# Folding the tokens a second time ahead of the channel DFT in an attention and Fourier-mix kernel

## Chip, cores and metric

The kernel runs on one core of a Trainium2 chip. The metric is the time of one execution on the device, in microseconds (us). The kernel before took 1283.77 us, the median of three runs (1283.46 to 1284.94).

## What is computed

Two blocks follow one another: attention with a hash mask, then a Fourier mix (FNet) with a small MLP. Cut to what matters:

```python
# attention, B, H, S, D = 4, 8, 768, 64; 6 hash bits
mask = q_bucket[..., :, None] == k_bucket[..., None, :]      # same hash bucket only
attn = softmax(where(mask, q @ k.T * scale, -1e9)) @ v

# bridge: (B, H, S, D) -> x of (B, S, 512)
X = fft(fft(x, axis=1), axis=2)                               # over tokens, then channels
u = x + real(X)
un = (u - mean(u)) / sqrt(var(u) + 1e-6)                      # over the 512 channels
out = u + maximum(un @ w_ch1, 0) @ w_ch2                      # 512 -> 2048 -> 512
```

The real part of the double transform needs sums with cosines and sums with sines only. Both are symmetric, so rows and columns can be added or subtracted in pairs ("folded") before a matmul, which makes the matmul smaller.

## The kernel before

The mix of batch b runs beside the attention of batch b + 1. Both are written as generators. An attention step (24 in a batch, 6 key blocks for each of 4 pairs of heads) is followed by three pieces of the mix. Batch 0's attention is emitted in a fixed order; later batches are ordered by a scheduler at compile time, which prefers what comes earlier in the program and fills an engine's gaps with later work. So the order of emission is a priority, and within one engine the final order is fixed at compile time. The mix of batch 3 has nothing beside it.

```python
def attention(b):
    ...
    for t in range(NPAIR):                       # 4 pairs of heads
        ...
        accs = [wt([P, 2, HALF], F32, "t3", f"acc{n}_{g}", 3) for g in range(2)]
        for c in range(NT):                      # 6 blocks of 128 keys
            new = [weigh(n, g, c) for g in range(2)]    # sc matmul, exp (ScalarE), mask (VectorE): pk
            if c == 0:
                first = new
            else:
                for g in range(2):               # the row sums: acc = pk + pk, acc + pk
                    nc.vector.tensor_tensor(accs[g], first[g][...] if c == 1 else accs[g], new[g][...], op=ALU.add)
            while pending:
                finish()                         # oo matmuls of the step before; after c = 5 the scaling of x
            ...
            yield

def mix(b):
    x = xs[b]
    z = wt([P, 2, 2, 2, HALF], F32, "z", f"z{b}", 1)
    for cp in range(2):                          # four pieces of fold
        for pc in range(2):
            e = wt([P, S], F32, "t3", f"e{b}_{cp}_{pc}", 3)
            nc.vector.tensor_tensor(e, x[:, cp], x[:, cp + 2], op=ALU.subtract if pc else ALU.add)
            for par in range(2):                 # s with s + 384: even and odd frequencies
                nc.vector.tensor_tensor(z[:, cp, pc, par], e[:, 0:HALF], e[:, HALF:S],
                                        op=ALU.subtract if par else ALU.add)
            yield
    hd = DM // 2
    F = wt([P, 2, NT // 2, 4 * hd], F32, "F", f"F{b}", 1)
    for par in range(2):
        for t in range(NT // 2):                 # channel DFT, 3 row blocks
            ps = pt([P, DM], f"cs{b}_{par}_{t}")
            for pc in range(2):
                for cp in range(2):
                    nc.tensor.matmul(ps[:, pc:DM:2], z[:, cp, pc, par, t * P : (t + 1) * P],
                                     ch[:, cp, pc, :], start=(cp == 0), stop=(cp == 1))   # 256 columns
            nc.scalar.copy(f[:, 0:DM], ps)
            nc.vector.tensor_copy(...)           # the mirrored half, read backwards
            yield
    ...
    for j in range(NDC):                         # sequence DFT
        pa, pb = (pt([P, HALF + 1], f"{nm}{b}_{j}") for nm in "AB")
        for par in range(2):
            for k, ps in enumerate((pa, pb)):
                for t in range(NT // 2):         # 3 row blocks
                    nc.tensor.matmul(ps[:, cols], f, sq[:, t, k, cols],
                                     start=(t == 0), stop=(t == NT // 2 - 1))
        ...                                      # x += A, x += or -= B
        yield
    ...                                          # h = relu(x @ w1), un (transposes), o = h @ w2

for b in range(B):
    if b > 0:
        for _ in attention(b):
            for _ in range(per_step):            # 3
                next(other, None)
    ...
    for _ in other:
        pass
    other, per_step = mix(b), 3
```

In what follows a piece is what runs from one `yield` of the mix to the next.

## Time and profile before

| | before |
|---|---|
| median of three runs | 1283.77 us |
| span of the profiled run | 1283.1 us |
| mean granted TensorE clock | 0.987 |
| idle time of TensorE (span less busy) | 61.5 us |

The page has a line with the granted clock in 40 slices of 32 us, in tenths of full speed (9 is 90% or more). This is the line of before:

```profile
PEclk9988999999999999999999999999999998999999
```

Every stretch of the clock in this trace is at 0.5 or 1.0, so an 8 is a slice with a few us at half clock. There are two in the first 130 us and one near 1080 us, after the last attention, and none beside the attention of batches 1 to 3. (A 9 can still hide a short stretch: the trace has half clock from 225.8 to 229.3.)

### The profile page before, as it was taken

The page shows a single profiled execution, that of the slowest core. Times are in us where ns is not written, and L with a number is a line of the kernel's source. Part 1 is how long each engine was busy: PE and PEld are TensorE (multiplying, and loading weights), DVE is VectorE, ACT ScalarE, POOL GpSimd, SP SyncE. Part 2 cuts the span into 40 slices and gives each one's busy share as a digit, 9 for nine tenths or more (in the row PEclk, how much of TensorE's full clock was granted, in tenths as well). Part 3 has the DMA queues.
Part 4 walks back from the last instruction along what each step waited for, and adds up shares of the span by engine and source line. Part 5 has one row for each costly group of instructions (what it writes and reads, how often), then busy time and mean ns, then how long its engine had stood idle before and what let it go on. Part 6 is the DMA issues. An engine that isn't in the chain of part 4 may idle for free.

```text
span 1283.1 us, 12028 instructions
## 1 busy us (share of the span) xinstructions
PE 1221.6 (95%) x4675; PEld 615.9 (48%) x4675; DVE 646.0 (50%) x1114; ACT 369.5 (29%) x631; POOL 129.8 (10%) x184
## 2 busy tenths in 40 slices
PE   6878898999999999999999999999999998999997
PEld 3333365444454446554455445744445444854553
DVE  3988888734446366443454448554434635311110
ACT  6875558521222132221222214122111211000000
POOL 2543015201001000000000100000000010001000
PEclk9988999999999999999999999999999998999999
DMA  9421225201101110010100101010000000000000
GB/s 291 115 63 38 50 78 168 61 6 29 33 1 25 29 33 14 13 25 9 33 21 13 33 9 46 1 25 13 21 17 1 1 17 9 1 1 17 9 8 19
DMA packets 82881, 44.65 MB, mean 35 GB/s; under 512 B 76800, under 2 KB 76928, under 8 KB 82688
## 3 DMA queue, kind: packets, MB, share of 16 engines
q1 hardware_dynamic: 74032, 23.61, 7.5%
q0 software_dynamic: 5648, 19.40, 4.7%
q10 hardware_dynamic: 3136, 0.79, 0.3%
q8 instruction: 39, 0.64, 0.2%
q14 instruction: 26, 0.21, 0.1%
HBM read 37.50 MB, written 6.29 MB: 34 GB/s over the span
## 4 chain that ended last, share of the span: by engine, by line
PE 78%; DVE 12%; DMA 3%; ACT 3%; issue 3%; POOL 0%; SPq 0%; ACTq 0%; POOLq 0%; DVEq 0%
PE h L974 25%; PE o L1002 25%; PE sc L789 9%; PE oo L809 7%; DVE pk L798 3%; PE cs L923 3%; DVE acc L868 3%; PE B L949 2%; PE A L949 2%; DMA zraw<-in_moe_w_ch_dram 2%; ACT pk L795 1%; PE sum L826 1%; DVE w L595 1%; PE un L990 1%; PE trk L701 1%
## 5 line engine op out<-in xcount | busy, mean ns | idle before, releaser
L974 PE MATMUL h<-x,w 128*128 128x384 f32 x1024 | 343.2, 492 | 9.2 <-DVE rt L832 3.9
L1002 PE MATMUL o<-w,h 128*128 128x512 f32 x768 | 342.1, 597 | 0.4 <-DVE h L981 0.4
L798 DVE SCALAR_TENSOR_TENSOR pk<-qb,kb,pk 128x384 f32<-128x384 bf16 x288 | 169.3, 626 | 194.1 <-ACT pk L795 194.1
L974 PEld LDWEIGHTS h<-x,w 128*128 128x128 f32 x1024 | 191.9, 191 | 156.4 <-issue 12.0
L795 ACT ACTIVATE pk<-sc 128x768 f32<-128x768 f32 x192 | 147.7, 808 | 310.3 <-PE sc L789 223.0
L1002 PEld LDWEIGHTS o<-w,h 128*128 128x128 f32 x768 | 141.5, 190 | 174.2 <-issue 167.7
L789 PE MATMUL sc<-qt,kt 64*128 64x384 f32 x768 | 187.5, 518 | 4.4 <-ACT pk L795 4.4
L809 PE MATMUL oo<-pk,vn 128*64 128x384 f32 (+1 forms) x768 | 157.5, 501 | 0.8 <-DVE pk L798 0.8
L868 DVE TENSOR_TENSOR acc<-acc,pk 128x768 f32<-128x768 f32 x128 | 133.3, 1052 | 10.1 <-ACT pk L795 8.3
L981 DVE TENSOR_SCALAR h<-h 128x384 f32<-128x384 f32 x64 | 35.6, 557 | 176.2 <-PE h L974 175.9
L789 PEld LDWEIGHTS sc<-qt,kt 64*128 64x128 f32 x768 | 76.7, 190 | 80.6 <-issue 50.2
L983 ACT ACTIVATE h<-h 128x384 f32<-128x384 f32 x64 | 31.3, 489 | 285.5 <-PE h L974 285.5
L809 PEld LDWEIGHTS oo<-pk,vn 128*64 128x64 f32 x768 | 48.9, 136 | 95.4 <-issue 79.2
L1008 DVE SCALAR_TENSOR_TENSOR u<-o,rs,u 128x512 f32<-128x512 f32 x24 | 18.0, 751 | 150.8 <-PE o L1002 122.5
L998 POOL TENSOR_SCALAR rs<-mv 128x1 f32<-128x1 f32 x24 | 6.5, 271 | 547.0 <-DVE mv L996 546.6
L893 POOL DMA_DIRECT2D out_dram<-u x32 | 19.6, 614 | 355.2 <-DVE u L1008 301.6
L923 PE MATMUL cs<-ch,z 128*128 128x256 f32 x192 | 47.7, 402 | 5.3 <-DVE z L910 3.7
L992 ACT COPY u<-un 128x512 f32<-128x512 f32 x24 | 14.1, 587 | 114.7 <-PE un L990 114.7
L923 PEld LDWEIGHTS cs<-ch,z 128*128 128x128 f32 x192 | 36.9, 199 | 17.9 <-DVE z L910 4.1
L949 PE MATMUL B<-sq,F 128*128 128x193 f32 (+1 forms) x192 | 37.0, 329 | 1.0 <-DVE F L930 0.6
L949 PE MATMUL A<-sq,F 128*128 128x193 f32 (+1 forms) x192 | 37.5, 330 | 0.0
L868 DVE TENSOR_TENSOR acc<-pk,pk 128x768 f32<-128x768 f32 x32 | 32.0, 1020 | 5.3 <-ACT pk L795 5.0
(109 smaller groups left out, 856.1 us busy)
## 6 DMA issues: line engine op xcount, KB each, us to landing
zraw<-in_moe_w_ch_dram POOLq DMA_DIRECT2D x21, 512.0 KB, 4.3
qn<-in_q_dram SPq DMA_DIRECT2D x32, 192.0 KB, 3.2
vn<-in_v_dram SPq DMA_DIRECT2D x30, 192.0 KB, 3.2
kn<-in_k_dram SPq DMA_DIRECT2D x30, 192.0 KB, 3.2
out_dram<-u POOLq DMA_DIRECT2D x16, 256.0 KB, 2.5
fraw<-in_moe_w_ch_dram SPq DMA_DIRECT2D x4, 512.0 KB, 7.2
fraw<-in_moe_w_ch_dram POOLq DMA_DIRECT2D x4, 512.0 KB, 4.2
out_dram<-u POOLq DMA_DIRECT2D x16, 128.0 KB, 2.4
```

What stands on the lines that cost most here:

```text
L789: nc.tensor.matmul(ps[:, h, 0:HALF], kt[rows, ks], qt[rows, qs], start=kb is not None, stop=True,)
L795: nc.scalar.activation(pk[:, :, 0:HALF], ps[:, :, 0:HALF], AF.Exp, scale=SCALE)
L798: nc.vector.scalar_tensor_tensor(pk[:, h, 0:HALF], qb[:, h, qs], kb[:, h, c : c + 1], pk[:, h, 0:HALF], op0=ALU.is_equal, op1=ALU.mult,)
L809: nc.tensor.matmul(oos[g][h * D : (h + 1) * D, 0:w], nat["v", n][:, c, h, :], pk[g][:, h, 0:w], start=(c == 0), stop=(c == NT - 1),)
L868: nc.vector.tensor_tensor(accs[g], first[g][:, :, 0:HALF] if c == 1 else accs[g], new[g][:, :, 0:HALF], op=ALU.add,)
L893: nc.gpsimd.dma_start(out[b, s0 : s0 + 2 * w - 1 : 2, :], src[at : at + w])
L923: nc.tensor.matmul(ps[:, pc:DM:2], z[:, cp, pc, par, t * P : (t + 1) * P], ch[:, cp, pc, :], start=(cp == 0), stop=(cp == 1),)
L949: nc.tensor.matmul(ps[:, cols], f, sq[:, t, k, cols], start=(t == 0), stop=(t == NT // 2 - 1),)
L974: nc.tensor.matmul(ps, w1[:, c, fc * P : (fc + 1) * P], x[:, c, g * HALF : (g + 1) * HALF], start=(c == 0), stop=(c == NDC - 1),)
L981: nc.vector.tensor_scalar(hr, ps, 0.0, None, op0=ALU.max)
L983: nc.scalar.activation(hr, ps, AF.Relu)
L1002: nc.tensor.matmul(ps, hs[fc][:, j * P : (j + 1) * P], w2[:, fc, :], start=(fc == 0), stop=(fc == NFC - 1),)
```

## The change

The intent is less TensorE work. After the fold of s with s + 384, the tokens are folded once more, s with 384 - s. A sum of cosines over both needs only f(s) + f(384 - s), one of sines only f(s) - f(384 - s). So the cosine rows and the sine rows become separate blocks: the sequence DFT contracts over two row blocks rather than three, and the channel DFT of a block that holds one kind computes 127 to 129 columns, not 256. The price is four small VectorE operations for each of the four fold pieces, with one operand read backwards, and a GpSimd copy of the rows that are their own partners (2 x 2 elements). Half of the fold (cp = 0: pairs 0 and 2) is called at a fixed place in the attention of pair 3; the mix keeps the other half, two pieces.

```diff
 (attention)
+            half = fold(b, 0) if t == NPAIR - 1 else iter(())
-            accs = [wt([P, 2, HALF], F32, "t3", f"acc{n}_{g}", 3) for g in range(2)]
+            accs = [wt([P, 2, HALF], F32, "t3", f"acc{n}_{g}", 4) for g in range(2)]
 ...
                 pending.append((n, c, new, oos, accs))
+                if c > 1:
+                    next(half, None)
 ...
+    def fold(b, cp):
+        x = xs[b]
+        if cp == 0:
+            zs[b] = wt([P, 2, 2, 2, HALF], F32, "z", f"z{b}", 1)
+        for pc in range(2):
+            e = wt([P, S], F32, "t3", f"e{b}_{cp}_{pc}", 4)
+            nc.vector.tensor_tensor(
+                e, x[:, cp], x[:, cp + 2], op=ALU.subtract if pc else ALU.add
+            )
+            f = wt([P, 2, HALF], F32, "t3", f"f{b}_{cp}_{pc}", 4)
+            for par in range(2):
+                nc.vector.tensor_tensor(
+                    f[:, par], e[:, 0:HALF], e[:, HALF:S],
+                    op=ALU.subtract if par else ALU.add,
+                )
+            z = zs[b][:, cp, pc]
+            n = HALF // 4 - 1
+            for at, op in ((0, ALU.add), (2 * n + 3, ALU.subtract)):
+                for i, first, last in ((0, 1, n), (n, 2 * n + 2, n + 1)):
+                    nc.vector.tensor_tensor(
+                        z[:, :, at + i : at + i + last], f[:, :, first : first + last],
+                        turned(f, 2 * n + 1 if i == 0 else HALF - 1, last), op=op,
+                    )
+            nc.gpsimd.tensor_copy(
+                z[:, :, 2 * n + 1 : 2 * n + 3], f[:, :, 0 : n + 2 : n + 1]
+            )
+            yield
 ...
     def mix(b):
         x = xs[b]
-        z = ...                                  # (the fold loop of before)
+        yield from fold(b, 1)
+        z = zs[b]
 ...
+                kinds = (0, 1) if t == 1 else (par ^ (t // 2),)
                 for pc in range(2):
+                    lo = 0 if 0 in kinds else hd // 2 + 1 - pc
+                    hi = hd if 1 in kinds else hd // 2 + 1 - pc
                     for cp in range(2):
                         nc.tensor.matmul(
-                            ps[:, pc:DM:2], z[:, cp, pc, par, t * P : (t + 1) * P],
-                            ch[:, cp, pc, :], start=(cp == 0), stop=(cp == 1),
+                            ps[:, pc + 2 * lo : pc + 2 * hi - 1 : 2],
+                            z[:, cp, pc, par, t * P : (t + 1) * P],
+                            ch[:, cp, pc, lo:hi], start=(cp == 0), stop=(cp == 1),
                         )
 ...
-                    for t in range(NT // 2):
+                    for t in range(2):
                         nc.tensor.matmul(
-                            ps[:, cols], f, sq[:, t, k, cols],
-                            start=(t == 0), stop=(t == NT // 2 - 1),
+                            ps[:, cols], F[:, par, k, t, j * P : (j + 1) * P],
+                            sq[:, t, k, cols], start=(t == 0), stop=(t == 1),
                         )
 ...
-            other = after(NPAIR + NT, other, weights(w2, moe_w_ch2))
+            other = after(2 + NT, other, weights(w2, moe_w_ch2))
```

The tables of constants, the copies into F and the zeroing of F's unused columns are adapted to the new blocks; they are cut here.

## The prediction

> **What bounds the kernel now.** I read, in order: busy times and slices, the groups by line and shape, the matmul timeline of the two stages that the change touches, busy times in short windows around the batch boundaries, and the timeline after the last attention.

> Engine shares, a line of the slices, and the two groups that the change shrinks (A has a twin, B):

> ```profile
> PE 1221.6 (95%) x4675; PEld 615.9 (48%) x4675; DVE 646.0 (50%) x1114; ACT 369.5 (29%) x631; POOL 129.8 (10%) x184
> ...
> DVE  3988888734446366443454448554434635311110
> ...
> L923 PE MATMUL cs<-ch,z 128*128 128x256 f32 x192 | 47.7, 402 | 5.3 <-DVE z L910 3.7
> ...
> L949 PE MATMUL A<-sq,F 128*128 128x193 f32 (+1 forms) x192 | 37.5, 330 | 0.0
> ```

> TensorE is busy 95% of the span, so work taken from it pays wherever nothing else holds that stage. VectorE's 50% is an average: 80 to 90% in the first 220 us, about 10% at the end. Each f32 matmul of the program is two records: the sequence stage issues 4 x 2 x 2 x 3 = 48 matmuls a batch, 192 in four, and A and B have 384 records. Below, "record" means such a half.

> A record's mean duration overlaps its neighbour's, so I take pitches from runs in the timeline:

> ```profile
> 478.26 3.72 PE L923 MATMUL cs<-ch,z 128*128 128x256 f32 x16 [0.21 <-ACT qt L517]
> ...
> 1093.74 1.14 PE L949 MATMUL A<-sq,F 128*128 128x192 f32 x6
> ...
> 1107.59 41.28 PE h L974 x128
> ```

> A record lasts 325 ns, six take 1.14 us, so the pitch is (1.14 - 0.325) / 5 = 0.163 us. The last line, from the chain, gives 41.28 / 128 = 0.3225 us for 384 columns. Both fit columns / 1.2 + 2.5 ns. For 256 columns that makes 216 ns; the trace has (3.72 - 0.38) / 15 = 223.

> Busy times in 5 us windows at the boundary of batches 1 and 2 (columns: TensorE, weight loads, VectorE, ScalarE, GpSimd, clock, DMA):

> ```profile
> 465.00:470.00 5.00, 4.67 (x23) 1.86 (x22) 4.76 (x14) 3.03 (x4) 0.00 (x0) 1.00 0.52 124
> 470.00:475.00 5.00, 5.00 (x24) 1.99 (x22) 5.00 (x10) 0.00 (x0) 0.00 (x0) 1.00 0.27 61
> 475.00:480.00 5.00, 3.59 (x15) 2.04 (x15) 5.00 (x10) 3.54 (x7) 0.00 (x0) 1.00 0.08 17
> 480.00:485.00 5.00, 5.00 (x26) 2.79 (x24) 5.00 (x9) 2.46 (x4) 0.00 (x0) 1.00 0.01 3
> 485.00:490.00 5.00, 5.00 (x21) 3.44 (x20) 4.66 (x8) 2.00 (x4) 0.29 (x2) 1.00 0.35 79
> 490.00:495.00 5.00, 5.00 (x27) 2.81 (x26) 1.63 (x4) 1.40 (x2) 0.00 (x0) 1.00 0.00 0
> ```

> From 465 to 490 VectorE is full: the scaling of pair 3, the fold, the first masks and sums of the next batch. TensorE still has work and loses only some 1.9 us. So the change takes TensorE work, and adds VectorE work, at the one place of a batch where both are near their limit.

> After the last attention nothing runs beside the mix (first TensorE, then VectorE, timeline):

> ```profile
> 1076.66 0.67 PE L923 MATMUL cs<-ch,z 128*128 128x256 f32 x2 [0.95 <-DVE mt L1060]
> 1078.69 1.83 DVE L906 TENSOR_TENSOR e<-x 128x768 f32<-128x768 f32 x2
> 1080.43 1.96 DVE L910 TENSOR_TENSOR z<-e 128x384 f32<-128x384 f32 x4
> 1081.04 10.90 PE L923 MATMUL cs<-ch,z 128*128 128x256 f32 x38 [3.71 <-DVE z L910]
> ```

> Only two e operations stand there, not four. The other two, on pairs 0 and 2, ran during pair 3's attention already (in batch 1 at 401.7 and 407.6, by the operations of tile e): the scheduler had filled VectorE gaps with them. So the "half beside pair 3" moves little; it mostly fixes the place.

> [...] after the 3.71 us wait above, the granted clock was 0.50 from 1081 to 1085. [...]

> **The change, part by part.**

> *Sequence DFT.* Three row blocks become two: 128 of 384 records go, 128 x 0.163 = **20.9 us of TensorE, 5.2 a batch**.

> *Channel DFT.* The pure blocks (two of three) need cosine or sine columns only: 128 of 192 records go from 256 to 127 to 129 columns. By the fit, 216 becomes 109 ns, 128 x 0.107 = **13.7 us, 3.4 a batch**. If weight loads at 190 ns set the pitch, it is only 128 x 0.026 = 3.3 us in all. I believe some 120 ns: 12.3 us, 3.1 a batch.

> *Second fold.* Per (cp, pc): before, e 0.95 and two z of 0.55, 2.05 us. After, e and two f the same, plus four operations on 2 x 95 or 2 x 96 elements, [...] ([...] two measured points give 0.353). Reversed reading seems free: the reversed 510-element F copy takes 687 ns[...]. So 3.47 us, +1.42; with four a batch +5.7, **+22.8 us of VectorE in all**. Half of it lies in pair 3, where VectorE has slack in batches 1 to 3; half at the boundary, +2.8.

> *Evictions.* 16 reversed F copies shrink from 510 to 255 elements, 0.687 to 0.42: -4.3 us VectorE, -1.1 a batch. [...] GpSimd's small copies and memsets stay near 0.2 us each.

> *Buffers and loads.* The table is a third smaller, 1155 to 770 KB, loaded while DMA is saturated: at about 400 GB/s 1 us of DMA, perhaps 0.5 us of time. The third work tile's space becomes a fourth buffer for f.

> TensorE loses 33 to 35 us, 2.6%; if all paid, 1250. By stage I expect less:
> - Batches 1 and 2: VectorE is full for 25 us, and after the change needs 2.8 - 1.1 = 1.7 more there, while the channel DFT waits for a fold that ends later. So the 3.1 us pay 0 to 2, the 5.2 pay. Together 5.5 each, **11**.
> - Batch 0: from 125 to 245 us VectorE, ScalarE and the second weight matrix's load and conversion bind (TensorE idles some 14 us), and part of the second fold delays pair 3 in a fixed order. I give **3** of 8.3.
> - Batch 3: before, last scaled x to first h is 1107.4 - 1078.7 = 28.7 us. After: fold 2 x 3.47 = 6.9, about 4.5 of channel DFT after it, partly at half clock, 64 x 0.163 = 10.4, some 1 of eviction: 22.8. **6**.
> - The mix now has 68 pieces, not 70, for 24 steps at three each, so the last attention step has none: **-1.5** over three batches. Start: **+0.5**.

> Sum 11 + 3 + 6 - 1.5 + 0.5 = 19: 1283.8 - 19 = **1265**.

> **Rivals.** (a) *All of it pays*: 1250. For it: TensorE is 95% busy, and the scheduler can pull later matmuls into gaps. Against it: 25 us of full VectorE, and the matmuls behind it need the whole channel result. (b) *VectorE becomes the bound at the boundaries*: the longer fold delays the channel DFT by all its 2.8 us in four batches and TensorE goes cold; gain 8 to 10, about 1275. For it: full windows and the halved clock after 1081; against: after 490 VectorE drops to a third, so delay is caught up. (c) *The halved channel matmuls are bound by weight loads*: 9 us less TensorE gain, some 3 us less time, 1268. (d) *The fixed fold in pair 3 stalls attention*: [...] the fold blocks it for 3.5 us, twice; four pk buffers hold two steps. In batches 1 to 3 the step has 11 us of other matmuls beside it; in batch 0 it has not, and 2 to 3 us could be lost.

> **Range and chances.** Between (a) and (b), with my sum in the middle: 1254 to 1275. Faster by over 2% means below 1258.1: it needs 26 us, three quarters of all TensorE savings. I give 0.24 to that, 0.75 to within 2%, 0.01 to slower.

> **What would show it.** Sequence matmuls 256 records at pitch 0.163; 128 channel records at 0.11 to 0.13 (0.16 to 0.19 under rival c); small fold operations at 0.35 us; VectorE total some 18 us up, TensorE some 30 down, and TensorE idle up by 10 or more, at the boundaries; the last x to first h at about 23 us. Wrong would be: idle not growing (rival a), or waits of the channel matmuls for z longer than 4 us at each boundary (rival b).

No term of the sum is among them: it came to 11 + 3 + 6 - 1.5 + 0.5 = 19 us, thus 1265. To support its terms, these numbers of before's trace:

- VectorE operations on f32 took 552 ns for 384 elements (z) and 948 for 768 (e). A straight line through both gives 353 ns for the 190 to 192 elements of a small operation, the estimate that still stands; four make 1.41 us, so that +1.42 and 3.47 stay within 0.01, and +22.8 within 0.2. For 255 elements it gives 0.42 us, and for 510 elements 682 ns, beside the 687 of the reversed copy. That reversed reading is free was an estimate at that time.
- The weight loads of A and B last 189 ns each, with the matmuls 163 ns apart, so the two overlap. The "some 120 ns" for a halved channel record is the estimate, between 109 by the fit and 190 by the loads.
- The half clock that goes with the wait of 3.71 us lasts from 1079.2 to 1086.0.
- From 20 to 30 us the DMA moves 410 GB/s at a share of 1.02. The 0.5 us at the start is an estimate, as are the 4.5 us for the channel DFT in batch 3.

## More of the kernel before

The boundary of batches 1 and 2 is where the change acts. VectorE's timeline of before (start, duration, engine, line, operation, tiles, count):

```profile
473.73 1.02 DVE L910 TENSOR_TENSOR z<-e 128x384 f32<-128x384 f32 x2
...
475.20 1.82 DVE L868 TENSOR_TENSOR acc<-pk,pk 128x768 f32<-128x768 f32 x2
...
477.50 0.94 DVE L906 TENSOR_TENSOR e<-x 128x768 f32<-128x768 f32 x1
```

The two parts of the fold that remain at the boundary are split: the first ends with z at 474.7, then come the sums (acc) of the next attention step, and only then the second part.

Last, one 10 us window of batch 0's end in before (columns: TensorE, weight loads, VectorE, ScalarE, GpSimd, clock, DMA share, GB/s):

```profile
140.00:150.00 10.00, 8.24 (x56) 3.51 (x54) 6.08 (x13) 5.14 (x9) 0.00 (x0) 1.00 0.18 40
```

## The result

| | before | after |
|---|---|---|
| median, four runs each | 1283.62 us (1283.19 to 1284.94) | 1280.62 us (1276.26 to 1280.88) |
| ratio | | 0.9967 (95%: 0.9944 to 0.9989) |
| span of the profiled run | 1283.1 us | 1279.0 us |
| mean granted TensorE clock | 0.987 | 0.969 |
| TensorE idle | 61.5 us | 67.9 us |

A ratio is the mean time of one kernel's fast runs over the mean of the other's of the same rounds, so it is not quite the ratio of the medians quoted beside it. The change stayed within 2%, the likeliest of the three outcomes predicted, but its time is 15.6 us above the 1265 predicted and 5.6 us above the top of the range.

The page of after, busy shares, the slices of VectorE and of the clock, and the channel group:

```profile
PE 1211.1 (95%) x4547; PEld 600.3 (47%) x4547; DVE 659.7 (52%) x1178; ACT 368.4 (29%) x639; POOL 145.2 (11%) x188
...
DVE  3988778833536457444444728654344646311110
...
PEclk9988889899999998999999998999999999999999
...
L970 PE MATMUL cs<-ch,z 128*128 128x128 f32 (+3 forms) x192 | 42.8, 381 | 10.6 <-DVE z L944 9.5
```

TensorE has 128 records fewer, as planned, yet its busy time fell only 10.5 us and not the 30 or more expected. The clock line tells why: beside slices 2 and 3 (counted from 0), which before has too, slices 4, 5, 7, 15 and 24 now show an 8. (The half clock after the last attention is still there, now spread over two slices.) A record at half clock takes twice as long and counts as busy all the while: in after the median pitch of 256-column records is 427 ns at 0.5 and 216 at 1.0, that of 384-column records (h) 640 and 323. The channel matmuls' waits for z have grown from 3.7 to 9.5 us.

The stage after the last attention went as foreseen (TensorE's timeline of after):

```profile
1084.90 8.14 PE L970 MATMUL cs<-ch,z 128*128 128x129 f32 x38 [5.11 <-DVE z L944]
...
1094.19 0.81 PE L999 MATMUL A<-sq,F 128*128 128x192 f32 x4
```

The sequence pitch is (0.81 - 0.325) / 3 = 0.162 us. The last scaled x to the first h took 28.7 us before and takes 21.9 us now (1081.4 to 1103.3).

To see where the rest went, I took the ends of the sum matmuls of each batch's pair 3 as marks, and the stretches between them. b0 is batch 0's mark.

| us | start to b0 | b0 to b1 | b1 to b2 | b2 to b3 | b3 to last o |
|---|---|---|---|---|---|
| before | 148.2 | 317.1 | 306.1 | 302.2 | 201.6 |
| after | 153.9 | 318.2 | 304.7 | 300.1 | 194.2 |
| gain | -5.7 | -1.1 | 1.4 | 2.1 | 7.4 |

So the last stage gains 7.4 us, the batch boundaries with attention beside them almost nothing, and batch 0 loses 6.8. The boundary of batches 1 and 2 in after, in 5 us windows with the columns as before:

```profile
475.00:480.00 5.00, 5.00 (x27) 1.93 (x24) 5.00 (x12) 1.46 (x2) 0.00 (x0) 1.00 0.00 2
480.00:485.00 5.00, 2.25 (x10) 0.86 (x8) 5.00 (x14) 0.00 (x0) 4.11 (x2) 1.00 0.00 0
485.00:490.00 5.00, 4.08 (x12) 2.01 (x11) 4.97 (x11) 3.30 (x6) 1.21 (x1) 0.52 0.20 45
490.00:495.00 5.00, 5.00 (x15) 3.93 (x14) 2.02 (x4) 0.90 (x4) 0.00 (x0) 0.50 0.15 34
```

From 480 to 485 TensorE is busy 2.25 of 5 us and ScalarE not at all, with VectorE full. Then the clock falls to 0.50 for ten us (485.2 to 495.5). VectorE's timeline in that window:

```profile
480.74 0.95 DVE L930 TENSOR_TENSOR e<-x 128x768 f32<-128x768 f32 x1
481.60 1.15 DVE L944 TENSOR_TENSOR z<-f 128x190 f32<-128x190 f32 x4
482.68 1.02 DVE L935 TENSOR_TENSOR f<-e 128x384 f32<-128x384 f32 x2
483.61 0.61 DVE L811 SCALAR_TENSOR_TENSOR pk<-qb,kb,pk 128x384 f32<-128x384 bf16 x1
484.14 1.15 DVE L944 TENSOR_TENSOR z<-f 128x190 f32<-128x190 f32 x4
485.21 0.95 DVE L882 TENSOR_TENSOR acc<-pk,pk 128x768 f32<-128x768 f32 x1
```

Here both remaining fold parts stand in a row, and acc comes after both. TensorE meanwhile (the wait before a group and who ended it stand in brackets):

```profile
482.27 0.71 PE L970 MATMUL cs<-ch,z 128*128 128x129 f32 x4 [1.46 <-DVE z L944]
484.28 0.86 PE L822 MATMUL oo<-pk,vn 128*64 128x384 f32 x2 [1.29 <-DVE pk L811]
...
486.67 0.90 PE L714 MATMUL trq<-ident,qn 128*128 128x128 f32 x3 [0.92 <-DVE F L983]
...
490.36 5.37 PE L970 MATMUL cs<-ch,z 128*128 128x256 f32 x16
```

Three waits of 1.46, 1.29 and 0.92 us, all ended by VectorE; the clock falls before the third. The 16 channel records after them take 5.37 us. The emission explains the order. With two fold pieces in place of four, and three pieces per attention step, both fold pieces and the first channel piece fall into the first step of the next batch, ahead of that batch's first acc (step c = 1). In before the last piece of fold fell into the second step, behind that acc.

Adding up the time at half clock, twice (1 - mean clock) times the span, gives 33 us before and 80 us after. The 47 more are worth up to 23 us, half of their length, if TensorE bounds them throughout; 2.7 of the 47 lie after the last work, so up to 22 are left. TensorE's work fell by 128 x 0.163 = 20.9 us and by 128 x some 0.104 = 13.3 us (223 ns before, about 119 now, measured below), in all 34. 34 less up to 22 for the clock and 6.4 for idle time leaves about 6; the span shows 4.1.

Around the end of batch 0's attention (153.9), whose order is fixed, 10 us windows of after:

```profile
140.00:150.00 10.00, 6.50 (x34) 2.64 (x36) 6.53 (x13) 4.08 (x7) 0.38 (x1) 0.69 0.01 3
...
170.00:180.00 10.00, 10.00 (x28) 6.25 (x28) 6.57 (x13) 4.84 (x10) 0.00 (x0) 0.60 0.18 41
```

In the first, TensorE is busy 1.7 us less than before in the same window and the clock halves at 143.9 for 6.8 us; at 167.8 it halves again, for 10.2 us. Before has neither. The second stretch is past b0, at the boundary of batches 0 and 1, and has the same waits for z and pk just before it, of 1.46 and 1.29 us.

### The profile page after: what moved, and what is told of

Its sections match the earlier page's. It is cut to its first block, busy times and chain, and to the rows that moved or that the text cites. A ratio compares the mean times of both kernels' runs of the same rounds, so it can differ in the third digit from the quotient of the medians.

```text
span 1279.0 us, 11866 instructions
## 1 busy us (share of the span) xinstructions
PE 1211.1 (95%) x4547; PEld 600.3 (47%) x4547; DVE 659.7 (52%) x1178; ACT 368.4 (29%) x639; POOL 145.2 (11%) x188
## 4 chain that ended last, share of the span: by engine, by line
PE 80%; DVE 12%; ACT 3%; issue 3%; DMA 1%; POOL 0%; SPq 0%; POOLq 0%; ACTq 0%; DVEq 0%
PE h L1024 25%; PE o L1052 25%; PE sc L802 10%; PE oo L822 8%; PE cs L970 3%; DVE acc L882 3%; DVE pk L811 2%; PE A L999 2%; PE B L999 1%; PE sum L839 1%; ACT pk L808 1%; DVE w L608 1%; PE un L1040 1%; PE trk L714 1%; DMA qn<-in_q_dram 1%
## 5 line engine op out<-in xcount | busy, mean ns | idle before, releaser
L802 PE MATMUL sc<-qt,kt 64*128 64x384 f32 x768 | 196.5, 532 | 0.0
L882 DVE TENSOR_TENSOR acc<-acc,pk 128x768 f32<-128x768 f32 x128 | 132.8, 1052 | 12.3 <-ACT pk L808 10.4
L802 PEld LDWEIGHTS sc<-qt,kt 64*128 64x128 f32 x768 | 79.3, 195 | 77.6 <-issue 51.9
L970 PE MATMUL cs<-ch,z 128*128 128x128 f32 (+3 forms) x192 | 42.8, 381 | 10.6 <-DVE z L944 9.5
L948 POOL COPY z<-f 128x4 f32<-128x4 f32 x16 | 19.9, 1245 | 120.2 <-DVE f L935 120.1
L613 POOL TENSOR_TENSOR w<-w,fraw 128x512 int32<-128x512 int32 x16 | 26.3, 1642 | 63.9 <-DVE w L608 25.8
```

The source lines that it names most:

```text
L613: nc.gpsimd.tensor_tensor(di, di, low, op=ALU.add)
L802: nc.tensor.matmul(ps[:, h, 0:HALF], kt[rows, ks], qt[rows, qs], start=kb is not None, stop=True,)
L882: nc.vector.tensor_tensor(accs[g], first[g][:, :, 0:HALF] if c == 1 else accs[g], new[g][:, :, 0:HALF], op=ALU.add,)
L970: nc.tensor.matmul(ps[:, pc + 2 * lo : pc + 2 * hi - 1 : 2], z[:, cp, pc, par, t * P : (t + 1) * P], ch[:, cp, pc, lo:hi], start=(cp == 0) ...
```

## The experiments

My theory after the two traces: the place of the fold in VectorE's order, fixed by where it is emitted, makes TensorE wait in short bunches; the bunches halve its clock; both together eat the gain. Rivals: the slow GpSimd copy holds z back; the added VectorE time itself does it wherever it stands; the halved channel matmuls gain less than their columns. Twelve kernels were run. All gave correct results. The ratios are against the kernel before, run on the same chip in the same rounds.

| label | what | median us | ratio (95%) | clock |
|---|---|---|---|---|
| (the change) | | 1280.62 | 0.9967 (0.9944 to 0.9989) | 0.969 |
| e1_act_copy | self-paired rows copied by ScalarE | 1279.16 | 0.9961 (0.9945 to 0.9978) | 0.974 |
| e2_no_early_half | both halves of the fold in the mix | 1263.72 | 0.9845 (0.9828 to 0.9863) | 0.983 |
| e3_full_channel | all 256 channel columns | 1287.06 | 1.0018 (1.0001 to 1.0035) | 0.977 |
| e4_hold_four | four pieces held back to the fold | 1248.78 | 0.9723 (0.9707 to 0.9739) | 0.984 |
| e5_pad | two empty pieces ahead of the fold | 1267.05 | 0.9864 (0.9848 to 0.9881) | 0.980 |
| e6_warm | filler matmuls beside the fold | 1271.74 | 0.9902 (0.9886 to 0.9919) | 0.985 |
| e7_noearly_hold4 | e2 and e4 together | 1251.37 | 0.9716 (0.9668 to 0.9764) | 0.981 |
| e8_before_hold4 | before, four pieces held back | 1268.53 | 0.9887 (0.9870 to 0.9903) | 0.989 |
| e9_noearly_hold4_warm0 | e7, fillers in batch 0 | 1248.12 | 0.9717 (0.9701 to 0.9734) | 0.986 |
| e10_noearly_hold8 | e2, eight pieces held back | 1239.81 | 0.9649 (0.9633 to 0.9665) | 0.980 |
| e11_double_small_folds | small fold operations issued twice | 1287.58 | 1.0028 (1.0011 to 1.0044) | 0.975 |
| e12_hold8_warm0_3 | e10, few fillers in batch 0 | 1241.24 | 0.9657 (0.9639 to 0.9675) | 0.986 |

The clock is that of the profiled run. The spans of the profiled runs between the marks (to about 0.1 us, one execution each), which the readings below use:

| us | start to b0 | b0 to b1 | b1 to b2 | b2 to b3 | b3 to last o |
|---|---|---|---|---|---|
| after | 153.9 | 318.2 | 304.7 | 300.1 | 194.2 |
| e1 | 152.0 | 317.9 | 304.7 | 300.1 | 194.2 |
| e2 | 149.2 | 312.7 | 300.5 | 296.5 | 194.5 |
| e3 | 154.2 | 318.2 | 304.3 | 303.5 | 197.1 |
| e5 | 150.9 | 314.6 | 300.4 | 296.5 | 194.5 |
| e6 | 153.2 | 313.0 | 302.7 | 298.2 | 195.1 |
| e11 | 155.5 | 318.9 | 306.4 | 302.2 | 194.4 |

### e1: is it the GpSimd copy?

```diff
-            nc.gpsimd.tensor_copy(
+            nc.scalar.copy(
                 z[:, :, 2 * n + 1 : 2 * n + 3], f[:, :, 0 : n + 2 : n + 1]
```

> Only edit: the copy of the two self-paired rows of z goes from GpSimd to ScalarE. In the changed kernel two such copies took 5.33 us together while VectorE was full. Rival 'GpSimd copy holds the mixed block': the channel matmuls start 2 to 3 us earlier at each of three boundaries, and with them the halved clock is shorter; total 1270 to 1274 us. My theory (VectorE's queue at the boundary and the halved clock after TensorE's idle gap): the channel matmuls wait for the z operations of VectorE, not for the copy, so 1279 to 1282 us, unchanged within 2 us.

Measured: 1279.16 us, 0.9961 beside the change's 0.9967. In after the copy of 128 x 4 elements took up to 2.86 us on GpSimd at the boundaries, and 0.30 to 0.38 in nine of its 16 cases, with VectorE busy beside both; on ScalarE it took 0.20 us at most. Still the stretches from b0 on moved by 0.3 us at most, so at the boundaries the copy is slow but not on the path, and this rival is out there. The stretch before b0 was 1.9 us shorter; whether by the copy or by the clock, which halved at other places, is open.

### e2: is it the place of the fold?

```diff
-            half = fold(b, 0) if t == NPAIR - 1 else iter(())
+            half = iter(())
 ...
+        yield from fold(b, 0)
         yield from fold(b, 1)
 ...
-            other = after(2 + NT, other, weights(w2, moe_w_ch2))
+            other = after(4 + NT, other, weights(w2, moe_w_ch2))
```

> Only edit: both halves of the fold stand in the mix again, none at a fixed place in pair 3. My theory: in batch 0 the fixed order delayed the end of pair 3 by 5.7 us (sum matmuls end at 153.9 instead of 148.2 us) and halved the clock for 6.8 us at 144; without it the end is back at 148 to 149 us. In the later batches the scheduler fills VectorE gaps with the first half as it did before the change, so little moves. Total 1272 to 1278. Rival (the early half helps, VectorE is the bound at the boundary and now gets 7 us more there): 1285 to 1300, with longer waits of the channel matmuls for z.

Measured: 1263.72 us, better than the theory's range. The same arithmetic with the four fold pieces in the mix gains 1.55% on before instead of 0.33%; the early half, with the two pieces fewer in the mix that go with it, costs 1.2%, some 16 us. VectorE's order at the boundary is that of before again:

```profile
472.85 1.81 DVE L882 TENSOR_TENSOR acc<-pk,pk 128x768 f32<-128x768 f32 x2
...
475.14 0.93 DVE L930 TENSOR_TENSOR e<-x 128x768 f32<-128x768 f32 x1
```

TensorE has one longer wait there and no cold stretch after it (timeline; then the window around the wait):

```profile
474.78 0.91 PE L802 MATMUL sc<-qt,kt 64*128 64x384 f32 x2 [2.00 <-ACT pk L808]
...
484.89 2.05 PE L971 MATMUL cs<-ch,z 128*128 128x127 f32 x16
```

```profile
470.00:475.00 5.00, 2.74 (x11) 0.89 (x10) 5.00 (x12) 1.75 (x3) 3.32 (x1) 1.00 0.35 79
```

The clock is 1.00 in this window, and the next three are full, also at 1.00. The run of 16 records also measures the halved channel matmul: (2.05 - 0.27) / 15 = 0.119 us each, with 0.27 for the last one. That is near the predicted 0.12, so the rival that weight loads hold them at 0.16 to 0.19 is out. And the fixed place was not needed for overlap: in e2 the scheduler itself ran the e operations of pairs 0 and 2 at 398.3 and 406.1, in pair 3's gaps.

Against before, e2's stretches gain -1.0, 4.4, 5.6, 5.7 and 7.1 us.

### e5: is it the bunching alone?

e2 moves both halves. Here the early half stays, and only the second half is moved back by two empty pieces:

```diff
+        yield
+        yield
         yield from fold(b, 1)
 ...
-            other = after(2 + NT, other, weights(w2, moe_w_ch2))
+            other = after(4 + NT, other, weights(w2, moe_w_ch2))
```

> Changed kernel with the early half kept in pair 3, and two empty pieces put ahead of the second half in each mix, so that the second half's two parts stand one attention step apart, as in the run without the early half (which gave 1263.7). Theory 'bunching': what cost the later batches was that the mix had two pieces fewer ahead of the second half, so that both its parts fell into the first attention step and delayed the masks and sums of the next; padding heals it: boundaries of batches 1 and 2 without half clock, total 1267 to 1272 (batch 0's delay of pair 3 stays). Rival 'the fixed place in pair 3 itself costs in every batch': total stays at 1277 to 1281.

Measured: 1267.05 us, ratio 0.9864. That is 1.03% of the 1.22% that e2 gains over the change. Two statements without any work take back some 13 of 16 us. VectorE's order at the boundary of batches 1 and 2:

```profile
475.36 1.15 DVE L944 TENSOR_TENSOR z<-f 128x190 f32<-128x190 f32 x4
476.43 1.82 DVE L882 TENSOR_TENSOR acc<-pk,pk 128x768 f32<-128x768 f32 x2
...
478.73 0.93 DVE L930 TENSOR_TENSOR e<-x 128x768 f32<-128x768 f32 x1
```

The sums stand between the two parts again, and neither boundary has half clock. Between b1 and b3 the stretches are those of e2 to 0.1 us; what is left lies in the first two stretches, thus in batch 0, where the early half stands in a fixed order. The empty pieces also move all later pieces of the mix back by two; e5 doesn't part this from the bunch.

### e6: how much of it is the clock?

TensorE is given work that computes nothing of use, 7 matmuls of 384 columns for each batch just ahead of the second half of the fold:

```diff
+        dummy = pt([P, HALF], f"dummy{b}")
+        for _ in range(7):
+            nc.tensor.matmul(dummy, ident, x[:, NPAIR - 1, HALF:S], start=True, stop=True)
         yield from fold(b, 1)
```

> Changed kernel with seven matmuls that compute nothing of use (identity times the scaled half of pair 3, 0.65 us each, 4.5 us of TensorE a batch) ahead of the second half of the fold, where TensorE idles. Theory 'half of the loss is the halved clock': the gap is filled, the clock stays at 1.0 from 485 to 495 us and from 789 to 799, which saves 5 us each, minus 1 to 2 us that the fillers delay others: total 1270 to 1275 though the kernel does more work. Rival (VectorE's queue alone is the cost, the clock only follows): 1280 to 1285.

TensorE's timeline and one window of e6:

```profile
472.26 4.78 PE L957 MATMUL dummy<-x,ident 128*128 128x384 f32 x14
```

```profile
475.00:480.00 5.00, 4.99 (x24) 2.89 (x22) 5.00 (x13) 0.38 (x1) 4.99 (x2) 1.00 0.00 0
```

The fillers add 4 x 14 x 0.3225 = 18 us of TensorE work, and the kernel is some 8 us faster (1271.74 us; 0.9902 against 0.9967). VectorE is as full as in after, the fold parts still stand together, but TensorE has no gaps and keeps its clock. Time at half clock, by the mean clock, falls from 80 to 38 us. No account of the waits alone makes added work pay, so a good part of the loss is the clock. The fillers also shift what stands beside the fold, so the split into waits and clock is not exact.

### e3: what are the halved channel matmuls worth?

```diff
-                    lo = 0 if 0 in kinds else hd // 2 + 1 - pc
-                    hi = hd if 1 in kinds else hd // 2 + 1 - pc
+                    lo = 0
+                    hi = hd
```

> Only edit: the channel matmuls stream all 256 columns again in every block (the sequence stage keeps its two blocks). That gives TensorE 128 records x 0.1 us = 13 us more work. If TensorE were the bound in that stage the total would rise by 10 to 13 us to 1290 to 1294. My theory says that TensorE idles or runs at half clock there, so that this work is nearly free in the three boundaries beside attention and costs about 3 us in the last batch: 1281 to 1286.

Measured: 1287.06 us, 0.5% above the change, thus 6.5 us for 13 us of TensorE work, slightly beyond my range. Two stretches, b0 to b1 and b1 to b2, did not grow at all, but in each of them e3 lacks a stretch of half clock, of 10.2 us, that after has. The window that goes with the cold one of after:

```profile
480.00:485.00 5.00, 2.67 (x12) 1.08 (x8) 5.00 (x14) 0.00 (x0) 3.84 (x2) 1.00 0.00 0
```

TensorE is again busy about half of the window, with ScalarE still, but here the clock stays at 1.00 from 257 to 789. The waits are the same three, of 1.46, 0.87 and 0.92 us. In the last two stretches, where both kernels had the same half clock (10.2 and 6.8 us), the columns paid 3.4 and 2.9 us, about all of the 3.3 us that a batch has of them. So they are not nearly free, as my theory had it: in the first two stretches the better clock can have hidden them. The rival that the halved matmuls gain less than their columns is out too.

| kernel | grid window, us | TensorE busy, us | clock after it |
|---|---|---|---|
| after | 478.40 to 481.81 | 2.41 | full |
| after | 481.81 to 485.22 | 1.65 | half |
| e3 | 478.73 to 482.15 | 2.35 | full |
| e3 | 482.15 to 485.56 | 2.15 | full |
| e2 | 470.77 to 474.19 | 1.75 | full |
| before | 475.02 to 478.43 | 2.00 | full |

So in these traces the fall goes not with the longest wait but with how little work falls into one window. The wider channel matmuls put 0.5 us more into e3's. The place of the grid goes into that count too: at the boundary of batches 2 and 3 the same waits leave after 0.71 us in 785.60 to 789.01, and e3 1.55 in 785.93 to 789.35, and both cool.

### e11: is it the amount of VectorE work?

```diff
-                    nc.vector.tensor_tensor(z[...], f[...], turned(...), op=op)
+                    for _ in range(2):
+                        nc.vector.tensor_tensor(z[...], f[...], turned(...), op=op)
```

> Changed kernel with each of the 64 small fold operations issued twice (same result): 22.8 us more of VectorE in all, half of it at the boundaries. If VectorE's queue at the boundary is what TensorE waits for, each boundary and the last fold lose their 2.8 us, batch 0's pair 3 2.8 more, and some windows of half clock grow: 1292 to 1302. If VectorE had slack there: under 1284.

Measured: 1287.58 us, 7 above the change. I had expected 1292 to 1302. In a row the 64 added operations cost less than 0.35 us each: eight take 2.23 us where four took 1.15, thus 1.1 us for each of 16 parts, 17 us in all and 2.2 at a boundary. The total hides some of it, as e11 had some 15 us less at half clock, by the mean clock. In the two stretches with the same half clock in both kernels (10.2 us each), b1 to b2 and b2 to b3, it grew by 1.7 and 2.1 us, for 2.2 us added at the boundary and 2.2 in pair 3. So a good part of VectorE's time there is on the path; if pair 3 hides its own share, nearly all of the boundary's. In the last stage the wait grew by 0.5 us and the channel run behind it, which starts at half clock, was shorter (7.83 us for after's 8.14):

```profile
1091.49 7.83 PE L971 MATMUL cs<-ch,z 128*128 128x129 f32 x38 [5.65 <-DVE z L945]
```

Still the place of the operations matters more than their number: in these two stretches the doubling costs 1.7 and 2.1 us, the bunch, against e2, 4.2 and 3.6.

### e4 and e8: work held back for the fold

If TensorE starves beside the fold, the mix of the batch before can leave something for it. Four pieces (32 records of o, 512 columns) are kept out of the attention steps and emitted between the fold pieces of the next mix:

```diff
-    def mix(b):
+    def mix(b, rest):
         x = xs[b]
-        yield from fold(b, 1)
+        for _ in fold(b, 1):
+            for _ in range(4 // 2):
+                next(rest, None)
+            yield
+        for _ in rest:
+            pass
 ...
-            for _ in attention(b):
-                for _ in range(per_step):
+            done = 0
+            for i, _ in enumerate(attention(b)):
+                while done < (68 - 4) * (i + 1) // (NPAIR * NT):
                     next(other, None)
+                    done += 1
 ...
-        for _ in other:
-            pass
-        other, per_step = mix(b), 3
+        other = mix(b, other)
```

> Edit: four pieces (one token block's 32 o records, 13.7 us of TensorE) of the mix of batch b - 1 are held back and emitted beside the fold of batch b; nothing else changes. My theory (TensorE lacks work while VectorE folds, cools to half clock for 10.2 us at the boundaries of batches 1 and 2 and 6.8 us in batch 3): clock stays at 1.0 at these three, each saves 5 to 8 us, total 1258 to 1267. Rival (VectorE's work at the boundary is the bound whatever TensorE does): the o matmuls only move, the boundary gets longer by what they take, total within 3 us of 1280.

TensorE's timeline of e4:

```profile
456.32 14.00 PE L1057 MATMUL o<-w,h 128*128 128x512 f32 x32 [0.59 <-DVE rt L845]
```

Measured: 1248.78 us, 0.9723, better than expected. 14 us of real work stand beside the scaling of pair 3 and both fold parts (VectorE runs them from 453 to 466, still in a row), and no half clock shows at the later boundaries. After the last attention it is the same: 32 held records run from 1040.1 to 1053.9, and the 48 channel records follow at once, without half clock. With 14 us of other TensorE work beside it the bunch does no harm here. One thing more than the holding changed: 64 pieces over 24 steps make two in the first step, not three, so the first channel piece falls behind the first acc. No run parts this from the work held back. In e8 below the first step also draws two pieces for three.

The same on the kernel before (70 pieces, one held piece after each fold piece) tells how much of this belongs to the change. Beside the same edit of the loop over batches, with 70 for 68:

```diff
-    def mix(b):
+    def mix(b, rest):
 ...
                         op=ALU.subtract if par else ALU.add,
                     )
+                next(rest, None)
                 yield
+        for _ in rest:
+            pass
```

> The kernel before the change, with four pieces of the former mix held back beside its single fold in the same way. My theory: before, TensorE idled only about 2 us at a boundary and kept its clock, so holding back gains little beside attention and some 5 to 7 us in the last batch: 1272 to 1279, and the second fold is worth 25 to 33 us once TensorE has work beside it. Rival (the holding alone is the gain, the second fold is worth nothing): 1250 to 1260.

Measured: 1268.53 us, 0.9887, better than expected too. Holding back is worth 1.1% without the second fold. Beside it the second fold is worth (0.9887 - 0.9723) of before, 1.6% or 21 us, where alone it is worth 0.3%. The TensorE work that it removes was there all along.

### e7, e9, e10, e12: towards a better version

e7 is e2 with four pieces held, one beside each of four fold pieces; e10 the same with eight held, two beside each:

```diff
-        yield from fold(b, 1)
+        for cp in range(2):
+            for _ in fold(b, cp):
+                for _ in range(4 // 4):          # e10: 8 // 4
+                    next(rest, None)
+                yield
+        for _ in rest:
+            pass
 ...
+                while done < (70 - 4) * (i + 1) // (NPAIR * NT):     # e10: 70 - 8
```

> Both cures: no early half, and four pieces of the former mix held back beside the fold. If they mend the same thing (TensorE without work at the boundary), they do not add up: 1244 to 1250, the 1248.8 of holding alone less the 3 to 5 us of batch 0's pair 3. If they mend different things they add: about 1232 to 1236.

e7 measured 1251.3 to 1251.9 in three runs and 1239.79 in one. The clock was 0.981 in the first three and 0.993 in the last. Two kinds of execution of one kernel, so whether the two cures add cannot be read from a median; neither kind lies in one of the two ranges expected. The profile fell in the slower kind and shows half clock from 164.3 to 184.8, in batch 0, where nothing can be held back.

> As the run with both cures (1251.4, one execution 1239.8), plus eight filler matmuls (5.2 us of TensorE) in batch 0 alone, ahead of its second half of the fold. In that run the profiled execution sat at half clock from 164 to 185 us in batch 0, right behind TensorE's idle at the fold; the fast one had a mean clock of 0.993 against 0.981. Theory: the fillers keep the clock, so all executions are near 1240 to 1245. Rival: the long half clock has another cause (the matmuls of the masks' stage are too sparse), and nothing changes or the fillers add their 5 us: 1250 to 1256.

e9 adds 8 filler matmuls, in batch 0 only, ahead of the second half of its fold:

```diff
+            if b == 0 and cp == 1:
+                dummy = pt([P, HALF], f"dummy{b}")
+                for _ in range(8):
+                    nc.tensor.matmul(dummy, ident, x[:, NPAIR - 1, HALF:S], start=True, stop=True)
```

It measured 1248.12 us (1246.97 to 1249.02). The long cold stretch is gone, and its four runs are of one kind, but the time missed the 1240 to 1245 expected, and the rival's range too. That the 5.2 us of fillers are paid, as batch 0 has little idle time in which to hide them, is likely but not shown.

> No early half, eight pieces (27 us of o matmuls) held back instead of four. Theory: four (13.7 us) already fill the 4 us of TensorE idle and the cooling at the boundary, so eight bring nothing beside attention and delay the next batch's channel DFT; 1248 to 1258. Rival (TensorE still lacks work with four): 1238 to 1246.

e10 measured 1239.1 to 1240.4 in four of six runs, and 1251.92 and 1250.75 in two, again with the clock apart: 0.989 to 0.993 against 0.980 and 0.985. My range was missed and the rival's held in most runs. (The ratio of 0.9649 is from its timed rounds; the mean of all six runs over before's median is 0.968.) A window of its profiled run, which was of the slower kind:

```profile
170.00:175.00 5.00, 5.00 (x10) 1.39 (x10) 1.96 (x3) 0.81 (x1) 2.01 (x1) 0.50 0.00 0
```

TensorE has records throughout and still the clock stays at 0.50, for 20.5 us from 165.0.

> As the run with eight pieces held back (1239.8 in most executions, 1251 to 1252 in two of six), plus three filler matmuls (2 us) in batch 0 ahead of the second half of the fold. If the slower executions come from TensorE cooling right there (half clock from 165 to 185.5 us in the profiled one), the fillers end them: all executions at 1240 to 1244. If not, two kinds of execution remain, near 1241 and 1253.

e12 is e10 with the fillers of e9 in batch 0, `range(3)` for `range(8)`. Six runs gave 1237.58 to 1242.97, median 1241.24, ratio 0.9657, with clocks of 0.986 to 0.992. None is near 1251, though two (1237.6 and 1237.9, clock 0.992) stand apart from four (1241.2 to 1243.0). Most executions of e10 are 1 to 2 us faster than this median. With fillers no execution of ten (e9, e12) was of the slower kind, without them (e7, e10) five of ten. It beats both kernels, before by 3.4% and the change by 3.1%.

## Why the prediction was right or wrong

**The TensorE work removed** was right: 128 records at 0.163 us, 128 at a saving of 0.104; 34 us against "33 to 35". Rival (c) fell with the measured 0.119.

**The small operations** were right: 0.349 us in the median against the 0.353 estimated from two operations that read forwards, so reading backwards showed no extra time. In a row they cost less: four take 1.15 us, not 4 x 0.353 = 1.41, so a fold part grew by some 1.15 and a boundary by 2.3 us, not 2.8. VectorE's busy time rose 13.7 us against some 18.

**The last stage** was right in mechanism and 1.4 us too careful: 7.4 us gained against 6, with 21.9 us from the last x to h against 22.8.

**Batches 1 and 2** were wrong: "Together 5.5 each" became 1.4 and 2.1. But e2, the same arithmetic in another place, gains 5.6 and 5.7 there. So the number was right for an order that this kernel doesn't have. Its split is another matter: it let 0 to 2 us of the channel columns pay, and in e3 they paid 3.4 where the clock was equal.

**Batch 0** was wrong in sign: 3 predicted, -6.8 measured over its two stretches, and again e2 gives what was predicted (-1.0 + 4.4 = 3.4).

**The step that failed** is therefore one sentence: 'So the "half beside pair 3" moves little; it mostly fixes the place.' It is true of the early half: the scheduler had run those operations in pair 3 anyway. It overlooked the other half. The mix now has two fold pieces, not four, and the prediction counted this only as a lost slot at the end ("-1.5 over three batches"). At the beginning it draws both pieces into one attention step, ahead of acc, on an engine whose order is fixed (in after acc runs at 485.2 us, behind the z operations of 484.1). e5 shows it with two empty pieces. Its companion, set against rival (b), failed too: "after 490 VectorE drops to a third, so delay is caught up". The delay was caught up on VectorE, but TensorE had lost its clock by then, until 495. The prediction had looked for long waits, and set the half clock from 1081 to 1085 beside before's wait of 3.71 us. But that clock fell at 1079.2, 1.8 us into the wait, after a grid window with 0.67 us of work; nor was before far from it at the boundary (2.00 of 3.41 us busy), where the prediction saw only "some 1.9 us" lost (its windows give 1.74).

**Rival (b)** had the right end, "TensorE goes cold", at 1275 and with the wrong cause, a long wait for z in proportion to the added 2.8 us. Its sign was to be "waits of the channel matmuls for z longer than 4 us at each boundary". None was longer than 1.5 at the boundary of batches 1 and 2: shorter waits, for z and pk, did it. Rival (d), the fixed order in batch 0, was priced at 2 to 3. e5, which keeps the early half in that order, is behind e2 by 1.7 and 1.9 us in batch 0's two stretches, 3.6 in all, so (d) was real and a little larger, though e5 also has 6.8 us more half clock than e2 in the second. Of the other 6.6 that after loses there against e2, 3.6 lie between b0 and b1, where the bunch stands. The other 3.0 lie before b0, where after and e5 run in the same order (compared from 125 us on), but after had 27.3 us at half clock and e5 20.5. That is no cost of the bunch.

The expected signs "TensorE some 30 down" and "idle up by 10 or more" were badly chosen. Busy time fell 10.5 and idle rose 6.4, because lost clock shows as busy time (640 ns for 323 from one h record to the next). The mean clock should have been among the signs.

In sum: 19 us expected; batch 0 misses it by 9.8, the two boundaries by 4.1 and 3.4, and the last stage gives back 1.4. The remaining 1.0 is the 1.5 and 0.5 for pieces and start, which cannot be told apart from the rest. That leaves the 4.1 that the spans show.

**Open.** Between 0.4 and 0.6 of a grid window the busy time alone does not decide (38 of 73 were followed by half clock); e7 and e9 both had 0.58 of a window busy in front of the fold of batch 0 (160.9 and 161.3 us), and only e7 cooled. The place of the grid differs from trace to trace; if it differs between executions of one kernel too, it may make the two kinds of e7 and e10, but only the slower kind was profiled. Why half clock lasted 20.5 us there, with TensorE busy, is open: most records of that stretch are attention matmuls with 64 rows or 64 columns of weights, but other windows of only such records were followed by full clock (after, 79.0 to 82.4). Of 113 grid windows at half clock in the 14 traces with TensorE busy for at least 0.95 of them, 96 were followed by full clock and 17 were not (before and after alone: 15 and 3 of 18; the 3 are one at each of after's boundaries). How e9 and e12 differ beyond the fillers' own time was not separated.

## What to carry to other kernels

When work is removed from the busiest engine, look at what else the edit moves: fewer pieces in an interleaved generator change which work stands ahead of which on an engine, and that can cost as much as the arithmetic saves (here some 16 us, e2 against the change). Read the mean granted clock beside the busy share, since lost clock hides as busy time: here TensorE was 95% busy before and after, with 33 and 80 us at half clock. Add up how much work falls into a few us, and don't look for the longest wait alone: here the clock fell after waits of 1.46 and 1.29 us that left 1.65 us of work in 3.41, and stayed after a wait of 2.00 us that left 1.75. And where the bound engine starves at a fixed place in a loop, keep back real work of the iteration before for that place: here this, with the change and a few fillers, took 3.4% off the kernel.
